# 55 matmuls of zeros between the first steps of a windowed-attention and feed-forward kernel

## The chip, the cores and the metric

The kernel runs on one core of one Trainium2 chip. The metric is the time of one execution in device microseconds; lower is better. The engines of the core are PE (matmuls; PEld is its weight load), DVE (vector), ACT (scalar, activations), POOL (GpSimd) and SP (which here only issues transfers). Each engine works through its own instructions in the order in which the program gives them, and waits on semaphores for the others.

## What is computed

```python
scores = (q @ k.T) / sqrt(64)                   # per batch (8) and head (8), 576 positions
scores = where(abs(i - j) <= 32, scores, -1e9)  # a window of 32 to each side
attn   = softmax(scores) @ v
x      = attn, heads side by side               # 4608 x 512
h      = x @ w_in                               # 512 x 2048
out    = max(0.01 * h, h) @ w_out               # 4608 x 512
```

## The kernel before

Attention is done in items: item i is one batch, one half of its positions (288) and one pair of heads (p), so eight items make a batch. An item goes around the engines like this: `score(i)` (PE, into the PSUM tile `ps`), `exps(i)` (ACT, reads `ps`, line 308), `masked(i)` (DVE or POOL, line 316), `sums(i)` (PE, into `s`, line 338), `inverse(i)` (DVE reciprocal, line 348), `product(i)` (PE, into `x`, line 363 in the first batch) and `scaled(i)` (DVE, into `xT`, line 387). Four items of one half make 288 columns of `xT` over all heads. On these the feed-forward part runs: `h_mms` (line 401) against `w_in`, the leaky ReLU on ACT (line 412), and `o_tile` (line 459) against `w_out`.

From the second batch on, a planner interleaves the attention of the next items with the matmuls of lines 401 and 459. The opening, that is the first batch, is written out by hand instead, line by line (525 to 649), and this list is the order of the instructions on every engine. In it the queries and keys of the first batch come in by eight transfers from the POOL queue (two for each pair of heads), are transposed by PE (`transpose_first`, line 208) and copied out by DVE or ACT (`evict_first`, line 143). The feed-forward part of the first half begins inside the opening: `h_chunk(c)` multiplies what `scaled(c)` has just finished, `h_open(f)` starts a further tile of 128 of the 2048 columns, and `h_close(f)` is its ReLU. With `h_first(1)` (line 651) the second half begins.

There is one `ps` tile, and every score uses it:

```python
ps = scps.tile([128, 1024], FP32)
P0 = 512 - HALF                                 # HALF is 288, so P0 is 224
by_n = ps[:, P0:P0 + 2 * HALF].rearrange("p (n t) -> p n t", n=2)  # score(i) writes here
nc.scalar.activation(out=e, in_=ps[:, P0:P0 + 2 * HALF], func=AF.Exp, scale=scale)  # exps
eng.memset(ps[:, 512:512 + HALF], 0.0)          # fill(V): columns 512 to 799
```

Columns 0 to 223 are read by nobody. `keep_busy(ps, 0, n)` writes there: n matmuls of the weights `ones_bd` with `busy`, a 128x224 tile of zeros (line 471). The kernel before calls it once, with 14, as PE's first work.

Of the kernel before, what the change touches and what calls it, by code (L numbers as in the profile page):

```python
# [16 lines left out]
def kernel(  # L17
# [91 lines left out]
    def load_v(b, p, engs=(nc.sync, nc.sync)):  # L109

        cast = engs[0] is nc.gpsimd
        if not cast:
            vf[b, p] = fload.tile([128, NB, D], FP32, name=f"vf{p}")
        for a, r in enumerate(HEADS):
            to = vf[b, p][r] if not cast else v0b[r, p] if b == 0 else vbd[b % 2][r, p, :, r]
            engs[a].dma_start(  # L116
                out=to, in_=v[b, 2 * p + a].rearrange("(c p) d -> p c d", p=64),
            )
# [68 lines left out]
    ps = scps.tile([128, 1024], FP32)  # L187
# [14 lines left out]
    def transpose_first(b, p, which):  # L202

        src = (q0b, k0b)[which == "k"]
        tp = mmps.tile([128, ROW, 64], BF16, name="tp", tag="mm")
        for c in range(ROW):
            for r in HEADS:
                nc.tensor.transpose(tp[r, c], src[r, p, c], ident[r, r])  # L208
        trans[b, p, which] = tp.rearrange("p c i -> p i c")

    def evict_first(b, p, which, eng):
        if which == "q":
            if b not in qT:
                qT[b] = attn.tile([128, NPAIR, S], BF16, name="qT")
            to = qT[b][:, p]
        else:
            to = kTs[b, p] = kt.tile([128, S], BF16, name="kT")
        copy_to(eng, to.rearrange("p (i c) -> p i c", c=ROW), trans.pop((b, p, which)))

    def value_first(b, p, eng):  # L220
        copy_to(eng, v0b[:, p], vf[b, p])
# [48 lines left out]
    def where(i):  # L270
        return i // 8, (i // 4) % 2, i % 4

    def score(i):
        b, hf, p = where(i)
        if b == 0:
            by_n = ps[:, P0:P0 + 2 * HALF].rearrange("p (n t) -> p n t", n=2)
            for n_, blocks in enumerate(WIN[hf]):
                for blk, i0, n in blocks:
                    lo, hi = 2 * i0, 2 * (i0 + n)
                    for r in HEADS:  # L280
                        nc.tensor.matmul(  # L281
                            by_n[r, n_, lo:hi], kTs[b, p][r, 64 * blk:64 * blk + 64],
                            qT[b][r, p, hf * HALF + lo:hf * HALF + hi], start=True, stop=True,
                        )
        elif b < NATURAL:
            by_n = ps[:, P0:P0 + 2 * HALF].rearrange("p (n t) -> p n t", n=2)
            for n_, blocks in enumerate(WIN[hf]):
                for blk, i0, n in blocks:
                    lo, hi = 2 * i0, 2 * (i0 + n)
                    nc.tensor.matmul(  # L290
                        by_n[:, n_, lo:hi], kbd[b % 2][:, p, blk],
                        qT[b][:, p, hf * HALF + lo:hf * HALF + hi], start=True, stop=True,
                    )
        else:
            by_c = qT[b][:, p].rearrange("p (c i) -> p c i", c=2)
            for n_, blocks in enumerate(WIN[hf]):
                for blk, i0, n in blocks:
                    nc.tensor.matmul(  # L298
                        ps_v[:, n_, :, i0:i0 + n], kbd[b % 2][:, p, blk],
                        by_c[:, :, hf * EVEN + i0:hf * EVEN + i0 + n], start=True, stop=True,  # L300
                    )
        if b > 0:
            exps(i)
            masked(i, nc.vector if i in ON_DVE else nc.gpsimd)

    def exps(i):
        e = attn.tile([128, 2 * HALF], BF16, name="e")
        nc.scalar.activation(out=e, in_=ps[:, P0:P0 + 2 * HALF], func=AF.Exp, scale=scale)  # L308
        probs[i] = e

    def masked(i, eng):
        b, hf, p = where(i)
        e = probs[i]
        pr = prob[:, i % NPROB]
        allowed = mask_first[hf] if b < NATURAL else mask[hf].rearrange("p n c i -> p n (c i)")
        eng.tensor_mul(  # L316
            pr.rearrange("p n c i -> p n (c i)"), e.rearrange("p (n t) -> p n t", n=2), allowed,
        )
        probs[i] = [pr, None, None, None]
# [9 lines left out]
    def sums(i):  # L329

        b, hf, p = where(i)
        pr, both = probs[i][:2]
        s = xps.tile([128, HALF], FP32, name="s")
        if both is not None:
            nc.tensor.matmul(s, ones_bd, both, start=True, stop=True)  # L335
        else:
            for n in range(2):
                nc.tensor.matmul(
                    s, ones_bd, pr[:, n].rearrange("p c i -> p (c i)"),
                    start=(n == 0), stop=(n == 1),  # L340
                )
        probs[i][2] = s
        if b > 0:
            inverse(i)
# [6 lines left out]
    def product(i):  # L351

        b, hf, p = where(i)
        pr = probs[i][0]
        x = xps.tile([128, HALF], FP32, name="x")
        x_v = x.rearrange("p (c i) -> p c i", c=2)
        flat = pr.rearrange("p n c i -> p n (c i)")
        parts = [(n_, *block) for n_ in range(2) for block in WIN[hf][n_]]
        if b == 0:
            for n_, blk, i0, n in parts:  # L360
                lo, hi = 2 * i0, 2 * (i0 + n)
                for r in HEADS:
                    nc.tensor.matmul(  # L363
                        x[r, lo:hi], v0b[r, p, blk], flat[r, n_, lo:hi],
                        start=(blk == parts[0][1]), stop=(blk == parts[-1][1]),
                        skip_group_check=True,
                    )
        else:
            for n_, blk, i0, n in parts:
                lo, hi = 2 * i0, 2 * (i0 + n)  # L370
                nc.tensor.matmul(  # L371
                    x[:, lo:hi] if b < NATURAL else x_v[:, :, i0:i0 + n], vbd[b % 2][:, p, blk, :],
                    flat[:, n_, lo:hi] if b < NATURAL else pr[:, n_, :, i0:i0 + n],
                    start=(blk == parts[0][1]), stop=(blk == parts[-1][1]),
                    skip_group_check=True,
                )
        probs[i][3] = x
# [7 lines left out]
    def scaled(i):  # L385
        r, x = probs.pop(i)[2:]
        nc.vector.tensor_mul(place(i), x, r)  # L387
# [28 lines left out]
    def h_chunk(c):  # L416
        for f in range(4):
            if c == 0:
                opened[f] = mmps.tile([128, 512], FP32, name="mm", tag="mm")
            h_mms(0, f, opened[f], (c,))  # L420

    def h_open(f):
        opened[f] = mmps.tile([128, 512], FP32, name="mm", tag="mm")
        h_mms(0, f, opened[f], range(DMC))

    def h_close(f):
        h_out(0, f, opened.pop(f))
# [39 lines left out]
    def keep_busy(t, lo, n, start=False):  # L467


        for _ in range(n):  # L470
            nc.tensor.matmul(
                t[:, lo:lo + 224], ones_bd, busy, start=start, stop=False,
                skip_group_check=True,
            )
# [42 lines left out]
    def load_w_in(f0, f1):  # L517
        nc.gpsimd.dma_start(out=w_in_bf[:, :, f0:f1], in_=w_in_r[:, :, f0:f1])
# [4 lines left out]

    V, G, A = nc.vector, nc.gpsimd, nc.scalar
    qT[0] = attn.tile([128, NPAIR, S], BF16, name="qT")
    keep_busy(ps, 0, 14, True)
    fill(V)
    transpose_first(0, 0, "k")
    evict_first(0, 0, "k", V)
    transpose_first(0, 0, "q")  # L530
    evict_first(0, 0, "q", A)
    transpose_first(0, 1, "k")
    score(0)
    evict_first(0, 1, "k", V)
    spread(A, GAP + 32, 2)
    load_v(0, 1, (G, G))
    transpose_first(0, 1, "q")
    exps(0)
    value_first(0, 0, V)
    transpose_first(0, 2, "k")  # L540
    evict_first(0, 1, "q", A)
    spread(V, 0, 3)
    masked(0, V)
    load_v(0, 2, (G, G))
    transpose_first(0, 2, "q")
    evict_first(0, 2, "k", V)
    sums(0)
# [3 lines left out]
    transpose_first(0, 3, "k")  # L551
    exps(1)
    load_v(0, 3, (G, G))
    transpose_first(0, 3, "q")
    evict_first(0, 3, "k", A)
    score(2)
# [3 lines left out]
    masked(1, V)  # L560
    exps(2)
    scaled(0)
    sums(1)
    load_w_in(512, 1024)
    score(3)
    inverse(1)
    product(1)
    masked(2, G)
    exps(3)
    score(4)  # L570
    masked(3, G)
    exps(4)
    scaled(1)
    sums(2)
    product(2)
    inverse(2)
    score(5)
    load_w_in(1024, 1536)
    exps(5)
    masked(4, G)  # L580
    score(6)
    scaled(2)
    sums(3)
    h_chunk(0)
    load_w_in(1536, 2048)
# [6 lines left out]
    h_chunk(2)  # L592
    load_w_out(0)
    scaled(3)
    sums(4)
    exps(7)
    h_chunk(3)
    inverse(4)
    masked(7, G)
    product(4)  # L600
    h_close(0)
    h_close(1)
    h_open(4)
    load_w_out(1)
    h_close(2)
# [164 lines left out]
```

## Time and profile before

| | |
|---|---|
| median of 3 runs | 317.73 us (317.68, 317.73, 318.78) |
| the profiled execution, its own time | 319.02 us |
| its span, first to last instruction | 317.3 us |
| what lies around the span | 1.7 us |
| mean granted TensorE clock over the span | 0.984 |
| busy, PE / DVE / POOL / ACT | 306.0 / 218.9 / 187.7 / 167.5 us |

Busy time of PE is modelled from pipelined matmuls, so a busy PE is not necessarily PE at its peak. A line of the timeline reads: start and length in us, engine, line of the kernel, operation, what it writes and reads, shape, count, and in brackets the idle time of the engine before it with what ended it. A window's line gives the busy time of each engine in that stretch, then the granted clock of PE (1.00 is full speed), then the mean share of busy transfer engines and GB/s.

### The profile page before, as it was taken

The page shows a single profiled execution, that of the slowest core. Times are in us where ns is not written, and L with a number is a line of the kernel's source. Part 1 is how long each engine was busy: PE and PEld are TensorE (multiplying, and loading weights), DVE is VectorE, ACT ScalarE, POOL GpSimd, SP SyncE. Part 2 cuts the span into 40 slices and gives each one's busy share as a digit, 9 for nine tenths or more (in the row PEclk, how much of TensorE's full clock was granted, in tenths as well). Part 3 has the DMA queues.
Part 4 walks back from the last instruction along what each step waited for, and adds up shares of the span by engine and source line. Part 5 has one row for each costly group of instructions (what it writes and reads, how often), then busy time and mean ns, then how long its engine had stood idle before and what let it go on. Part 6 is the DMA issues. An engine that isn't in the chain of part 4 may idle for free.

```text
span 317.3 us, 6932 instructions
## 1 busy us (share of the span) xinstructions
PE 306.0 (96%) x2692; PEld 204.6 (64%) x2714; DVE 218.9 (69%) x267; ACT 167.5 (53%) x370; POOL 187.7 (59%) x258
## 2 busy tenths in 40 slices
PE   5889999999999999999999999999999999999996
PEld 4657755674755858585765858576765858576653
DVE  2879758699765996788655997688755988565100
ACT  2636755472743828274652828375552837464531
POOL 8989984536356866686546866686647866330000
PEclk9579999999999999999999999999999999999999
DMA  7999999969997994499635995599733450000102
GB/s 130 136 183 207 206 144 237 200 157 235 223 193 184 213 215 118 100 241 208 149 74 152 212 229 134 75 225 232 163 76 107 110 68 35 34 35 1 66 24 77
DMA packets 107313, 46.09 MB, mean 145 GB/s; under 512 B 68752, under 2 KB 102800, under 8 KB 107280
## 3 DMA queue, kind: packets, MB, share of 16 engines
q1 hardware_dynamic: 91936, 37.91, 58.3%
q0 software_dynamic: 14752, 7.59, 18.1%
q8 instruction: 21, 0.34, 0.5%
q10 hardware_dynamic: 592, 0.15, 0.2%
q14 instruction: 12, 0.10, 0.1%
HBM read 36.70 MB, written 9.44 MB: 145 GB/s over the span
## 4 chain that ended last, share of the span: by engine, by line
PE 77%; POOL 10%; DVE 5%; DMA 4%; issue 2%; ACT 1%; SPq 0%; DVEq 0%; ACTq 0%; POOLq 0%
PE mm L459 33%; PE mm L401 33%; PE x L371 4%; PE ps L298 3%; DVE r L348 2%; DMA kf<-in_k_dram 2%; POOL vbd L657 2%; PE s L335 2%; POOL vbd L116 2%; DMA qb<-in_q_dram 2%; POOL prob L316 2%; POOL kb L99 1%; POOL qb L99 1%; PE ps L281 1%; DVE both L326 1%
## 5 line engine op out<-in xcount | busy, mean ns | idle before, releaser
L348 DVE RECIPROCAL r<-s 128x288 f32<-128x288 f32 x64 | 125.2, 1956 | 53.3 <-PE s L335 50.7
L401 PE MATMUL mm<-xT,w_in_bf 128*128 128x288 bf16 x1024 | 135.0, 288 | 0.1
L459 PE MATMUL mm<-w_out_bf,gT 128*128 128x512 bf16 (+2 forms) x570 | 129.5, 373 | 1.3 <-issue 0.2
L412 ACT ACTIVATE gT<-mm 128x288 bf16<-128x288 f32 x256 | 101.5, 410 | 27.1 <-PE mm L401 10.3
L401 PEld LDWEIGHTS <-w_in_bf 128*128 128x128 bf16 x1024 | 98.6, 98 | 25.7 <-issue 0.5
L316 POOL TENSOR_TENSOR prob<-e,mask 128x576 bf16<-128x576 bf16 x48 | 61.3, 1278 | 83.8 <-issue 40.7
L459 PEld LDWEIGHTS <-gT 128*128 128x128 bf16 x592 | 55.8, 98 | 58.0
L464 ACT ACTIVATE o_sb<-mm 128x512 f32<-128x512 f32 (+2 forms) x37 | 21.7, 586 | 91.1 <-PE mm L459 91.1
L308 ACT ACTIVATE e<-ps 128x576 bf16<-128x576 f32 x64 | 41.4, 647 | 17.9 <-PE ps L298 7.4
L387 DVE TENSOR_TENSOR xT<-x,r 128x288 bf16<-128x288 f32 x64 | 29.2, 457 | 7.1 <-PE x L363 0.9
L235 POOL CAST vbd<-vf 64x576 bf16<-64x576 f32 x48 | 33.1, 690 | 1.4
L262 DVE COPY kbd<-kT 64x576 bf16<-64x576 bf16 x48 | 31.2, 650 | 0.3
L230 POOL CAST kb<-kf 96x384 bf16<-96x384 f32 x48 | 27.1, 590 | 1.8 <-DMA kf<-in_k_dram 1.8
L230 POOL CAST qb<-qf 96x384 bf16<-96x384 f32 x48 | 24.4, 535 | 4.4 <-DMA qf<-in_q_dram 3.9
L326 DVE TENSOR_TENSOR both<-prob 128x288 bf16<-128x288 bf16 x52 | 21.7, 417 | 3.2 <-POOL prob L316 2.5
L371 PE MATMUL x<-prob,vbd 128*128 128x96 bf16 (+1 forms) x280 | 22.6, 212 | 0.6 <-DVE xT L387 0.6
L371 PEld LDWEIGHTS <-vbd 128*128 128x128 bf16 x280 | 18.0, 98 | 3.8 <-DVE xT L387 0.7
L298 PEld LDWEIGHTS <-kbd 128*128 128x128 bf16 x240 | 15.5, 98 | 6.9
L298 PE MATMUL ps<-qT,kbd 128*128 128x128 bf16 (+2 forms) x240 | 19.3, 212 | 0.0
L335 PE MATMUL s<-both,ones_bd 128*128 128x288 bf16 x52 | 14.9, 286 | 0.2
L316 POOL TENSOR_TENSOR prob<-e,wide 128x576 bf16<-128x576 bf16 x8 | 10.2, 1276 | 5.3 <-ACT e L308 5.1
L141 ACT ACTIVATE qT<-tp 128x576 bf16<-128x576 bf16 x7 | 4.5, 649 | 7.4 <-PE tp L208 7.4
(51 smaller groups left out, 110.4 us busy)
## 6 DMA issues: line engine op xcount, KB each, us to landing
out_dram<-o_sb SPq DMA_DIRECT2D x35, 256.0 KB, 3.9
vf<-in_v_dram SPq DMA_DIRECT2D x49, 144.0 KB, 3.5
qf<-in_q_dram SPq DMA_DIRECT2D x24, 288.0 KB, 4.3
kf<-in_k_dram SPq DMA_DIRECT2D x24, 288.0 KB, 4.7
w_in_bf<-in_moe_w_in_dram POOLq DMA_DIRECT2D x4, 512.0 KB, 8.1
w_out_bf<-in_moe_w_out_dram POOLq DMA_DIRECT2D x4, 512.0 KB, 8.8
kb<-in_k_dram POOLq DMA_DIRECT2D x4, 144.0 KB, 4.6
qb<-in_q_dram POOLq DMA_DIRECT2D x4, 144.0 KB, 4.8
```

What stands on the lines that cost most here:

```text
L230: nc.gpsimd.tensor_copy(out=dst[:, p, 3 * c:3 * c + 3], in_=by_c[c])
L235: nc.gpsimd.tensor_copy(out=vbd[b % 2][r, p, :, r], in_=vf[b, p][r])
L262: nc.vector.tensor_copy(out=to.rearrange("p n (m c) -> p n c m", c=2), in_=kT[r].rearrange("p (c n m) -> p n c m", c=2, n=NB),)
L298: nc.tensor.matmul(ps_v[:, n_, :, i0:i0 + n], kbd[b % 2][:, p, blk], by_c[:, :, hf * EVEN + i0:hf * EVEN + i0 + n], start=True, stop=True,)
L308: nc.scalar.activation(out=e, in_=ps[:, P0:P0 + 2 * HALF], func=AF.Exp, scale=scale)
L316: eng.tensor_mul(pr.rearrange("p n c i -> p n (c i)"), e.rearrange("p (n t) -> p n t", n=2), allowed,)
L348: nc.vector.reciprocal(r, probs[i][2])
L371: nc.tensor.matmul(x[:, lo:hi] if b < NATURAL else x_v[:, :, i0:i0 + n], vbd[b % 2][:, p, blk, :], flat[:, n_, lo:hi] if b < NATURAL else ...
L387: nc.vector.tensor_mul(place(i), x, r)
L401: nc.tensor.matmul(h[:, 0:HALF], w_in_bf[:, c, ts(f, 128)], xT[:, c, ds(g * HALF % RING, HALF)], start=(c == 0), stop=(c == DMC - 1),)
L412: nc.scalar.activation(out=to, in_=x, func=AF.Prelu, alpha=0.01)
L459: nc.tensor.matmul(o[:, lo:hi], gT[:, f, ds(128 * j % RING, 128)], w_out_bf[:, f, lo:hi], start=(f == 0), stop=(f == FFC - 1),)
```

## The change

The first call of `keep_busy` issues 17 matmuls instead of 14, and sixteen further calls with 55 matmuls in all stand between steps of the hand-written opening. These calls leave `start` at False. Nothing else changes its place. In order:

```diff
-    keep_busy(ps, 0, 14, True)
+    keep_busy(ps, 0, 17, True)
     fill(V)
     transpose_first(0, 0, "k")
     evict_first(0, 0, "k", V)
+    keep_busy(ps, 0, 3)
     transpose_first(0, 0, "q")
     evict_first(0, 0, "q", A)
+    keep_busy(ps, 0, 4)
     transpose_first(0, 1, "k")
     score(0)
...
+    keep_busy(ps, 0, 6)
     transpose_first(0, 1, "q")
     exps(0)
     value_first(0, 0, V)
+    keep_busy(ps, 0, 5)
     transpose_first(0, 2, "k")
...
+    keep_busy(ps, 0, 3)
     transpose_first(0, 2, "q")
     evict_first(0, 2, "k", V)
     sums(0)
     evict_first(0, 2, "q", A)
     score(1)
     inverse(0)
     transpose_first(0, 3, "k")
     exps(1)
     load_v(0, 3, (G, G))
+    keep_busy(ps, 0, 3)
     transpose_first(0, 3, "q")
     evict_first(0, 3, "k", A)
     score(2)
     product(0)
...
     exps(2)
     scaled(0)
+    keep_busy(ps, 0, 6)
     sums(1)
     load_w_in(512, 1024)
+    keep_busy(ps, 0, 1)
     score(3)
     inverse(1)
     product(1)
     masked(2, G)
     exps(3)
+    keep_busy(ps, 0, 4)
     score(4)
     masked(3, G)
     exps(4)
     scaled(1)
+    keep_busy(ps, 0, 4)
     sums(2)
+    keep_busy(ps, 0, 1)
     product(2)
     inverse(2)
     score(5)
     load_w_in(1024, 1536)
     exps(5)
     masked(4, G)
+    keep_busy(ps, 0, 6)
     score(6)
     scaled(2)
+    keep_busy(ps, 0, 3)
     sums(3)
     h_chunk(0)
     load_w_in(1536, 2048)
     exps(6)
     inverse(3)
     h_chunk(1)
     masked(5, G)
     score(7)
     product(3)
     h_chunk(2)
     load_w_out(0)
     scaled(3)
+    keep_busy(ps, 0, 2)
     sums(4)
     exps(7)
+    keep_busy(ps, 0, 1)
     h_chunk(3)
...
     h_close(1)
+    keep_busy(ps, 0, 3)
     h_open(4)
```

## The prediction

> **What bounds the kernel now.** I read the page first: the busy shares and the chain of waits.
>
> ```profile
> PE 306.0 (96%) x2692; PEld 204.6 (64%) x2714; DVE 218.9 (69%) x267; ACT 167.5 (53%) x370; POOL 187.7 (59%) x258
> PE 77%; POOL 10%; DVE 5%; DMA 4%; issue 2%; ACT 1%; SPq 0%; DVEq 0%; ACTq 0%; POOLq 0%
> ```
>
> PE is busy 96% of the span and makes up 77% of the chain. Windows of 5 us show it busy for 4.79 to 5.00 us in each from 20 to 50 us, so little later can absorb a late opening: what PE loses before 22 us is lost at the end. Next the windows, cut where the granted clock changes (the last but two columns: clock, DMA share, GB/s; PE busy stands first).
>
> ```profile
> 1.51:4.93 3.42, 2.80 (x14) 1.94 (x14) 0.60 (x4) 1.28 (x1) 3.35 (x8) 1.00 0.91 169
> 4.93:8.34 3.41, 1.93 (x80) 1.54 (x82) 1.34 (x2) 0.95 (x2) 3.15 (x9) 1.00 1.08 154
> 8.34:11.76 3.42, 2.55 (x62) 1.76 (x56) 2.40 (x6) 1.84 (x4) 3.42 (x6) 0.50 1.54 168
> 11.76:15.17 3.41, 3.41 (x82) 2.78 (x80) 3.08 (x4) 2.33 (x5) 2.90 (x4) 0.50 1.45 91
> 15.17:18.58 3.41, 1.79 (x42) 1.17 (x39) 3.31 (x3) 1.90 (x3) 3.25 (x4) 1.00 1.20 192
> 18.58:22.00 3.42, 3.42 (x28) 2.08 (x29) 2.78 (x3) 0.65 (x1) 3.31 (x4) 0.50 1.10 164
> ```
>
> The clock moves in steps of 3.41 us, and each stretch follows how busy PE was in the one before: after 57%, 75% and 52% busy it is half, after 82% (the zeros of line 471) and 100% it is full. (The first stretch is shown as 1.00, but its 14 matmuls of 224 columns start 0.187 us apart, against 0.1225 for 288 columns at full clock, 36 in 4.41 us in the chain: it ran at half.) So work of zeros does count, and three half stretches lie in the opening. The last, full of work, costs 1.7 us.
>
> Then the timelines of PE, ACT and DVE, for what each wait is and what may be put into it.
>
> ```profile
> 14.41 0.66 PE L281 MATMUL ps<-qT,kT 64*64 64x96 bf16 x10
> 15.82 0.43 PE L281 MATMUL ps<-qT,kT 64*64 64x64 bf16 x10 [0.40 <-ACT e L308]
> 16.53 0.42 PE L338 MATMUL s<-prob,ones_bd 128*128 128x288 bf16 x2 [0.29 <-DVE r L348]
> 18.56 0.66 PE L281 MATMUL ps<-qT,kT 64*64 64x64 bf16 x10 [0.80 <-ACT e L308]
> ```
>
> ```profile
> 13.67 0.67 ACT L308 ACTIVATE e<-ps 128x576 bf16<-128x576 f32 x1
> 15.12 0.65 ACT L308 ACTIVATE e<-ps 128x576 bf16<-128x576 f32 x1 [0.78 <-PE ps L281]
> 16.34 0.65 ACT L308 ACTIVATE e<-ps 128x576 bf16<-128x576 f32 x1 [0.58 <-PE ps L281]
> 17.86 0.65 ACT L308 ACTIVATE e<-ps 128x576 bf16<-128x576 f32 x1 [0.87 <-PE ps L281]
> ```
>
> ```profile
> 4.51 0.30 DVE L224 MEMSET ps<- 128x288 f32 x1 [1.02 <-PE ps L471]
> ```
>
> The last line decides this case. `fill` writes columns 512 to 799 of `ps`, the zeros columns 0 to 223, and still `fill` waits for the last of the zeros: accesses to `ps` are ordered by the tile, not by its columns. So zeros that stand behind `exps(i)` in the program must wait until ACT has read `ps`, and an `exps` behind zeros must wait for them. They don't run in the waits for ACT, they run after them.
>
> [...]
>
> **The change, part by part.** A matmul of zeros costs 0.187 us at half clock; at full, 0.1225 x 224/288 = 0.095. Going from 64-row to 128-row matmuls and back costs about 0.1 each (10.76 to 11.36 us: two sums of 0.24 each take 0.60 before the next score).
>
> The bare round is from one `exps` to the next: 0.65 of ACT, 0.05 to the score, 0.52 from the score's start to the next `exps`, 1.22 in all, which is 15.12 to 16.34. At full clock the zeros then make of it:
> - 2 to 3: 6 zeros 0.57, a switch 0.1, `sums(1)` 0.25, 1 zero and a switch 0.19: 2.25 to 2.35, against 1.45 now. `sums(1)` did not have to wait for `exps(2)` before.
> - 3 to 4: 4 zeros and a switch 0.48: 1.70, against 1.22.
> - 4 to 5: 0.48, `sums(2)` 0.25, a zero and switches 0.3, `product(2)` 0.24: 2.3, against 1.52. Here `sums(2)`, which ran beside `exps(4)`, is pushed behind it.
> - 5 to 6: 6 zeros and switch 0.67, and 3 zeros with two switches before `sums(3)`, for which `exps(6)` must now wait, 0.4: 2.3, against 1.46.
>
> The four rounds lose 0.85 + 0.48 + 0.78 + 0.84 = 2.95 us. Ahead of them: the three more at the start end at 4.56 + 0.39, before the first transpose at 5.00 (and `fill` ends at 5.37, before DVE's copy at 5.51): nothing. The 3 and 4 before `q` of pair 0 and `k` of pair 1 lie in waits of 0.26 and 1.05 us for their transfers: nothing to 0.1. The 6, 5, 3 and 3 up to `score(2)` cost 17 x 0.095 = 1.6 plus switches, of which the waits for transfers (0.78 before 9.37) and a full clock for 8.34 to 13 give back most: `exps(2)` comes 0.4 late. Behind them: the two chunks from 19.61 at full clock rather than half give back 8 x 0.12 = 0.95; the 2 before `sums(4)` hold up `exps(7)`, and the 1 behind it waits for `exps(7)`, where `h_chunk(3)` waited for nothing: 0.65 us of ACT and 0.1; the 3 before `h_open(4)` lie in its wait for a buffer, 0 to 0.3. Sum: 0.4 + 2.95 - 0.95 - 0.5 (`product(3)` and the next, at full clock too) + 0.75 = 2.65 us, with a full clock throughout.
>
> That is the floor; it won't be held. A round of 2.3 us leaves PE idle for about 0.8 (ACT's 0.65 and the ways there and back), so it is 65% busy, below the 75% after which the clock was half. At half clock the same round is 2.3 + 7 x 0.09 + 0.4 = 3.3, and 76% busy: between 75% and 82%, so undecided. Half and full will take turns. A half stretch costs 3.41 x 0.76 / 2 = 1.3 us; I count two of them behind 13 us (the floor has taken back those of before): 2.65 + 2.7 = 5.3 us. Bounds: none (2.65), all of them (four or five more, +9).
>
> Nothing else pays for it or hides it: no transfer moves in its queue, though POOL's `load_w_in` and `load_w_out` stand behind `masked` on POOL and come later with it, by as much as PE.
>
> Against its own execution (319.02 us) this is 324.3. The median, 317.73, lies 1.3 below that execution, and one run in three was at 318.78: where the 3.41 us steps fall differs between executions. I take the shift at the median and forecast 323.0 us; own range 320.3 to 327.
>
> **Rivals.**
> - The clock stays full (2.65 alone): 320.4. The zeros add work to each stretch, and 82% was enough. [...]
> - Nearly always half: each stretch from 13 us on stays below what is needed, since PE stands still in every `exps`. 326.7.
> - Absorbed: PE's later waits (1.46 us idle from 20 to 80 us) shrink and only 1 us is left: 318.8. Against it: those pieces are 0.2 to 0.45 us, and follow PE's own order.
> - Faster: the zeros do not wait for `exps`, as the line of `fill` would have to be a peculiarity of the first call. Then PE is fed in its waits of 0.40, 0.29 and 0.80 us, the clock is full from 8.34 us, the half stretches give back 1.7 (the last) and little from the first two (9.37 and 10.14 us wait for transfers); the zeros that overhang cost some 0.3 to 0.5. 316.4 us. It decides at one point: whether zeros behind `exps(2)` start before ACT ends. That the change does nothing at all can't be: 58 matmuls are 5.5 us at full clock and PE waits for some 4.2 us in all before 19 us.
>
> **How the numbers follow.** Main case 0.52; clock full 0.22; nearly always half 0.13; absorbed 0.07; faster 0.06. 0.5% (1.6 us), about what a measurement of this kernel can tell from no change, puts the limits at 316.1 and 319.3. Faster by more: half of the last case, 0.03. Within: the other half, the absorbed case, and 0.02 of the full clock on an unlucky reference, 0.12. Slower: 0.85. The range 319.4 to 327.0 leaves out the faster and absorbed cases and the top of the half-clock case.
>
> **What would show it.** In the changed profile zeros stand directly behind the end of each `exps`, with PE idle before them "<-ACT e"; the starts of the third to sixth `exps` lie 1.7 to 3.3 us apart; `sums(2)` waits for zeros, not for the reciprocal; the granted clock still shows half stretches after 8.34 us; `h_chunk(0)` begins 3 to 6 us later than 19.61. It is wrong if zeros overlap with an `exps` on ACT, or if the clock is 1.00 from 8.34 us on with `h_chunk(0)` before 19.6.

## The result, and the profile after

The changed kernel takes 321.71 us (median of 5, 321.66 to 322.86) against 317.80 for the kernel before: a ratio of 1.0129 with a 95% interval of 1.0106 to 1.0152, so slower by about 1.3%. The profiled execution took 321.70 us with a span of 320.0 (before: 319.02 and 317.3). Executions more than 1.5% above the fastest of their kernel are called slow and left out of the ratios below; among them are e2's profiled one (1814.88 us) and three of e4's six, its profiled one (329.99 us) included.

The forecast of 323.0 was of the right sign and the result lies in its range, but it got there by a term that is not there: the clock.

From the page of the changed kernel, the granted clock in 40 slices; nothing in it is below 9 (before: 9, 5, 7, 9 at the start). Its record begins at 4.36 us; the zeros ahead of that start 0.187 us apart, against 0.095 from 9.21 us on, so they ran at half.

```profile
PEclk9999999999999999999999999999999999999999
```

Two of its stretches of 3.41 us, in which PE was busy for only 2.17 and 2.11 us (64% and 62%), with the full one that follows the first (the stretch behind the second, from 21.42 us, is full too):

```profile
11.19:14.60 3.41, 2.17 (x71) 1.78 (x70) 2.73 (x3) 2.92 (x5) 2.69 (x4) 1.00 1.65 101
14.60:18.01 3.41, 2.58 (x43) 2.02 (x43) 2.26 (x2) 0.85 (x2) 2.45 (x2) 1.00 1.14 172
18.01:21.42 3.41, 2.11 (x33) 1.66 (x32) 2.13 (x3) 1.10 (x2) 3.38 (x5) 1.00 1.20 187
```

The timeline of PE in the changed kernel, over three rounds:

```profile
14.62 0.74 PE L471 MATMUL ps<-busy,ones_bd 128*128 128x224 bf16 x6 [0.80 <-ACT e L308]
15.20 0.41 PE L338 MATMUL s<-prob,ones_bd 128*128 128x288 bf16 x2
15.44 0.26 PE L471 MATMUL ps<-busy,ones_bd 128*128 128x224 bf16 x1
15.63 0.43 PE L281 MATMUL ps<-qT,kT 64*64 64x96 bf16 x10
16.80 0.54 PE L471 MATMUL ps<-busy,ones_bd 128*128 128x224 bf16 x4 [0.50 <-ACT e L308]
18.51 0.54 PE L471 MATMUL ps<-busy,ones_bd 128*128 128x224 bf16 x4 [0.80 <-ACT e L308]
18.89 0.41 PE L338 MATMUL s<-prob,ones_bd 128*128 128x288 bf16 x2
```

PE is idle first, until ACT has read `ps`, and only then come the zeros, with the useful work behind them. The waits were not filled, and `sums(1)` and `sums(2)`, which did not wait for ACT before, now stand behind zeros that do. The list of waits (us in total, times, longest) has both directions, seven groups of zeros that wait for `exps` and two `exps` that wait for zeros:

```profile
PE ps L471 <- ACT e L308: 4.3, 7, 0.8
ACT e L308 <- PE ps L471: 3.6, 2, 2.0
```

The timeline of ACT in the changed kernel; these are `exps(2)` to `exps(7)`:

```profile
13.93 0.65 ACT L308 ACTIVATE e<-ps 128x576 bf16<-128x576 f32 x1
16.10 0.65 ACT L308 ACTIVATE e<-ps 128x576 bf16<-128x576 f32 x1 [1.53 <-PE ps L281]
17.81 0.65 ACT L308 ACTIVATE e<-ps 128x576 bf16<-128x576 f32 x1 [1.06 <-PE ps L281]
20.10 0.65 ACT L308 ACTIVATE e<-ps 128x576 bf16<-128x576 f32 x1 [1.64 <-PE ps L281]
22.39 0.65 ACT L308 ACTIVATE e<-ps 128x576 bf16<-128x576 f32 x1 [1.64 <-PE ps L471]
25.00 0.65 ACT L308 ACTIVATE e<-ps 128x576 bf16<-128x576 f32 x1 [1.97 <-PE ps L471]
```

The rounds are 2.17, 1.71, 2.29 and 2.29 us long. At the end of the opening the delay is handed on whole. The line to compare is the eighth and last reciprocal of the first batch in DVE's timeline, before and then after:

```profile
31.17 1.96 DVE L348 RECIPROCAL r<-s 128x288 f32<-128x288 f32 x1 [0.15 <-PE s L338]
```

```profile
33.80 1.96 DVE L348 RECIPROCAL r<-s 128x288 f32<-128x288 f32 x1
```

From its start to the end of the span it is 286.15 us before (317.31 - 31.17) and 286.17 after (319.97 - 33.80). So the opening alone decides, and the start of this one instruction tells what it lost: 2.63 us.

### The profile page after: what moved, and what is told of

Its sections match the earlier page's. It is cut to its first block, busy times and chain, and to the rows that moved or that the text cites. A ratio compares the mean times of both kernels' runs of the same rounds, so it can differ in the third digit from the quotient of the medians.

```text
span 320.0 us, 7048 instructions
## 1 busy us (share of the span) xinstructions
PE 308.4 (96%) x2750; PEld 207.7 (65%) x2772; DVE 219.3 (69%) x267; ACT 167.8 (52%) x370; POOL 187.7 (59%) x258
## 4 chain that ended last, share of the span: by engine, by line
PE 78%; POOL 9%; DVE 5%; DMA 3%; issue 3%; ACT 1%; SPq 0%; ACTq 0%; DVEq 0%; POOLq 0%
PE mm L459 33%; PE mm L401 32%; PE x L371 4%; PE ps L298 3%; POOL vbd L673 2%; DVE r L348 2%; DMA kf<-in_k_dram 2%; PE s L335 2%; PE ps L471 2%; POOL prob L316 2%; POOL vbd L116 2%; ACT e L308 1%; DMA kb<-in_k_dram 1%; POOL w_out_bf L522 1%; DVE both L326 1%
## 5 line engine op out<-in xcount | busy, mean ns | idle before, releaser
L471 PE MATMUL ps<-busy,ones_bd 128*128 128x224 bf16 x72 | 11.1, 287 | 5.8 <-ACT e L308 4.3
```

## The experiments

The table gives the start of that last reciprocal, the span, and the difference, all from the profiled execution. The time is the median of the executions that the ratio uses; ratios are to the kernel before in the same job.

| kernel | us | ratio, 95% interval | last reciprocal | span | span less reciprocal |
|---|---|---|---|---|---|
| before, first profile | 317.73 | | 31.17 | 317.31 | 286.15 |
| changed | 321.71 | 1.0129, 1.0106 to 1.0152 | 33.80 | 319.97 | 286.17 |
| e1, only groups behind an `exps` | 321.02 | 1.0098, 1.0077 to 1.0118 | 33.02 | 319.19 | 286.17 |
| e2, only the other groups | 317.90 | 1.0013, 0.9987 to 1.0039 | | | |
| e3, zeros in other tiles | 319.20 | 1.0036, 1.0018 to 1.0053 | 30.95 | 317.51 | 286.56 |
| e4, a quarter of the array | 328.18 | 1.0286, 1.0232 to 1.0341 | 42.14 | 328.29 | 286.15 |
| e5, before again | 317.58 | 0.9994, 0.9977 to 1.0011 | 30.95 | 317.11 | 286.16 |
| e6, sums ahead of the zeros | 321.45 | 1.0121, 1.0104 to 1.0138 | 34.01 | 320.18 | 286.17 |
| e7, fewer zeros, in other tiles | 317.62 | 0.9995, 0.9984 to 1.0006 | 30.09 | 316.24 | 286.15 |
| e8, e2 again | 320.05 | 1.0068, 1.0049 to 1.0088 | 31.19 | 317.35 | 286.16 |
| e9, groups behind an `exps` doubled | 325.25 | 1.0221, 1.0195 to 1.0247 | 37.77 | 323.94 | 286.17 |
| e10, one zero in each of these groups | 320.93 | 1.0097, 1.0061 to 1.0133 | 31.94 | 318.09 | 286.15 |

**e1 and e2: which groups carry the loss.** The calls of the changed kernel are divided in two; both keep the first 17.

```diff
-    keep_busy(ps, 0, 3)  # e1: out, with the 4, 6, 3, 1, 1, 3, 2 and 3 that are not behind an exps
     keep_busy(ps, 0, 5)  # e1: stays, with 3, 6, 4, 4, 6 and 1; e2 has it the other way round
```

> The first call of 17 and, of the others, only the seven groups (29 zeros) that stand behind an exps in the program: 5, 3, 6, 4, 4, 6 and 1. Theory A (the loss is new waits of zeros for ACT's exps, in each round): these seven carry it, and more than half of the 3.9 us stays: with the clock full, rounds of 2.15, 1.7, 2.0 and 1.9 us, 319.8 us; idle time of PE before line 471 ended by ACT e about 4 us as in the changed kernel. Rival B (every zero costs its own 0.095 us, wherever it stands): 29 of 58 zeros, so half of 3.9, 319.8 us too, but PE's idle time ended by ACT e would not be what changes against the kernel before. The two part in the next kernels.

> The first call of 17 and only the other ten groups (26 zeros), none of them the first thing behind an exps that is still running. Theory A: they lie in waits for transfers or cost at most their own time off the chain: 317.4 us with a full clock, up to 1.5 more if half stretches come back. Rival B: half of 3.9 us stays, 319.7.

e1 keeps 3.2 of the 3.9 us with 29 of the 55 zeros of the new calls. Its rounds, from `exps(2)` to `exps(6)`, are 2.08, 1.71, 2.19 and 1.90 us, close to what was expected; the 319.8 us was 1.2 too low, and in its profile the clock was half once, from 8.69 to 12.10 us. At its median e2 is not to be told from the kernel before. That a zero costs its own time wherever it stands (rival B, 319.7 for e2) is out. e2 is less clean than its median looks: its executions spread from 317.2 to 321.5, it has no profile that can be used, and e8, below, is the same kernel.

**e3: the same zeros, another tile.** From the fourth group on the zeros go into spare columns of the tiles of `sums` and `product`, each at a point where no other engine reads that tile.

```diff
-        s = xps.tile([128, HALF], FP32, name="s")
+        s = spare("s", i)[:, 0:HALF]      # a tile of 512 columns; x in the same way
...
-    keep_busy(ps, 0, 4)
+    keep_busy_in("x", 1, 4)               # keep_busy(spare("x", 1), HALF, 4, True)
     score(4)
```

> All 58 zeros at the same places of PE's order, but from the fourth group on they go into spare columns 288 to 511 of the tiles s and x, which no engine reads at that time, so that no zeros wait for an exps and no exps for zeros. Theory A: the loss is gone, exps at most 1.5 us apart from the third to the seventh, 317.4 us. Rival B: the zeros still take 58 x 0.095 us of PE, 321.7 us or a little less.

319.20: most of the loss is gone, 1.4 us are not. No zeros wait for an `exps` in its profile, against 4.3 us in the changed kernel. The rounds are 1.50, 1.23, 1.90 and 1.23 us; the third is longer than the 1.5 expected, so the placing costs something of its own. One such cost shows on DVE (line 481 is the zeros' line here): `scaled(2)` must wait for the three zeros that went into its `x` ahead of `sums(3)`, and DVE stands idle for 0.71 us before it:

```profile
19.91 0.46 DVE L397 TENSOR_TENSOR xT<-x,r 128x288 bf16<-128x288 f32 x1 [0.71 <-PE x L481]
```

The zeros here also set `start`; that flag was not tested by itself. Another 0.41 us lie behind the opening (286.56 against 286.15), where PE waits 0.33 us at 40.82 for a transfer into `kb`.

**e7: the cleaner contrast.** Of e3's zeros only those groups stay that stood behind an `exps`, 25 of the 29 of e1, in the same places of PE's order; the start has 17 + 3 + 4 as in the changed kernel.

```diff
-    keep_busy_in("x", 2, 3)               # before scaled(2); so the 6, 3, 3, 1, 1, 2, 1 and 3
     keep_busy_in("x", 2, 6)               # stays before score(6), with 5, 6, 4 and 4
```

> The first 17 + 3 + 4 zeros in ps as in the changed kernel, then only 5, 6, 4, 4 and 6 in spare columns of s and x; dropped are the 6 before q of pair 1, the 3 before q of pairs 2 and 3, all single ones, and those before sums(3), sums(4) and h_open(4), among them the 3 that scaled(2) had to wait for. Theory A1: the 1.4 us that the kernel with all zeros elsewhere still lost were delays of the chain of reciprocals by such zeros; clock full, 317.0 to 317.8 us. Rival (the zeros of the seven groups cost their own PE time even where they wait for nothing): 318.6 us or more.

317.62, and 0.9995 (0.9984 to 1.0006): the loss is gone, as theory A1 had it; which of the dropped zeros cost e3 its 1.4 us was not parted further. PE in e7, the round from `exps(3)` (which runs from 14.65 to 15.30) to `exps(4)`:

```profile
14.44 0.41 PE L373 MATMUL x<-prob,v0b 64*64 64x96 bf16 x10
14.78 0.56 PE L481 MATMUL x<-busy,ones_bd 128*128 128x224 bf16 x4
15.35 0.43 PE L281 MATMUL ps<-qT,kT 64*64 64x64 bf16 x10
```

Here the four zeros run beside ACT, and the score follows 0.05 us behind the end of `exps(3)`; in the changed kernel the same four started 0.05 us after ACT's end. In e7, too, no zeros wait for an `exps`. Against e1 the difference is 3.4 us. That is nearly all for which tile the zeros write to, but not a pure measure of it: e1 has four zeros more behind an `exps` and lacks the 3 and 4 of the start. Its half stretch is not what parts the two, since the two executions of e1 with a mean clock of 1.000 (321.12 and 321.35 us) are no faster than the others.

**e9 and e10: the price of one zero.** The seven groups are doubled, and cut to one each.

```diff
-    keep_busy(ps, 0, 6)
+    keep_busy(ps, 0, 12)                  # e9; e10: keep_busy(ps, 0, 1)
     sums(1)
```

> The changed kernel with the seven groups behind an exps doubled (5, 3, 6, 4, 4, 6, 1 become 10, 6, 12, 8, 8, 12, 2): 29 zeros more. Theory A2 (each of these zeros lies on the chain of rounds from exps to exps, at 0.095 us): 2.75 us more at most, the 5 and the 3 partly covered by transfers, so 2.0 to 2.75: 323.7 to 324.5 us, last reciprocal 36 to 36.6 us, clock full. Rival (they lie beside DVE's reciprocals, and only the wait for ACT costs): 321.7 us.

> The changed kernel with one zero matmul in each of the seven groups behind an exps, 22 fewer; the other groups stay. The waits for ACT stay, the zeros' own time goes. Theory A2: 22 x 0.095 = 2.1 us less, 319.6 us with a full clock; with half stretches (theory C: less of the array at work) up to 1.7 more. Rival (only the wait costs): 321.7 us with a full clock.

The group of six that took 0.74 us at 14.62 in the changed kernel, in e9 with twelve, behind the same wait:

```profile
16.59 1.31 PE L471 MATMUL ps<-busy,ones_bd 128*128 128x224 bf16 x12 [0.80 <-ACT e L308]
```

In e9 the four rounds are 2.75, 2.09, 2.67 and 2.86 us: longer by 0.58, 0.38, 0.38 and 0.57 for 6, 4, 4 and 6 zeros, about 0.095 each, as the prediction put it. The time rose by 3.5 us rather than 2 to 2.75. The rounds give 1.91 of it; most of the rest lies ahead of them, for the first reciprocal starts at 13.10 instead of 11.43. There the clock of the profile was half up to 6.59 us, and five zeros more stand ahead of `k` of pair 2; how the two share it was not parted. In e10 the rounds are 1.69, 1.42, 2.00 and 1.80, shorter by 0.48, 0.29, 0.29 and 0.49 for 5, 3, 3 and 5 zeros. Its three executions with a mean clock of 1.000 took 319.83, 319.97 and 320.44 us, near the 319.6 expected; the three below 1.000 took 321.42 to 322.94. That only the wait costs is out: zeros and waits both do.

**e6: DVE's reciprocals or the rounds?** The same 58 zeros, but `sums(1)`, `sums(2)` and `sums(3)` go ahead of the zeros that stood before them.

```diff
-    keep_busy(ps, 0, 6)
     sums(1)
     load_w_in(512, 1024)
-    keep_busy(ps, 0, 1)
+    keep_busy(ps, 0, 7)
     score(3)
```

> The changed kernel with the same 58 zeros, but in three places sums(i) goes ahead of the zeros that stood before it: 7 zeros behind sums(1), 5 behind sums(2), 3 behind sums(3). No zeros leave PE's order, and the rounds from exps to exps stay as long. Theory A1 (what sets the end of the opening is DVE's chain of reciprocals, started late by sums that wait for exps): inverse(1) starts at 14.5 instead of 15.64, the last reciprocal 2 us earlier than 33.80, 319.7 us. Theory A2 (the rounds of PE and ACT themselves set it): unchanged, 321.7 us.

321.45, so A1 fell. From the first to the second reciprocal it is indeed 2.82 us rather than 4.21, but from the first to the last it is 21.88 against 22.37 (compared from the first, which comes 0.70 later here, with the clock half up to 7.13 us): the later `sums` stand behind `score(4)` and `score(6)` in PE's order, and these keep waiting for the lengthened rounds. So the rounds of PE and ACT set the pace.

**e4: the zeros on a quarter of the array.** They use 64x64 of it, for the same number of columns.

```diff
-                t[:, lo:lo + 224], ones_bd, busy, start=start, stop=False,
+                t[0:64, lo:lo + 224], ones_bd[0:64, 0:64], busy[0:64], start=start, stop=False,
```

> All groups as in the changed kernel, but each matmul of zeros uses 64 x 64 of the array (rows and columns 0 to 63) instead of 128 x 128, and so a quarter of it, for the same 224 columns. What the prediction missed is the full clock from 4.36 us on. Theory C (the gate counts how much of the array works): a quarter of the activity, half stretches come back, and 322.5 to 325 us. Theory D (it counts only the time in which PE is fed): clock 1.000 and 321.7 us, some tenths less for fewer switches between 64-row and 128-row matmuls.

The three executions that the ratio uses took 324.47, 328.18 and 328.54 us, the last two above the 322.5 to 325 that theory C gave; these two show recorded half stretches (mean clock 0.990 and 0.984). The profile is of an execution of 329.99 us. Its timeline of PE has the group that took 0.54 us at 18.51 in the changed kernel, behind the same wait:

```profile
22.86 0.90 PE L471 MATMUL ps<-busy,ones_bd 64*64 64x224 bf16 x4 [0.81 <-ACT e L308]
```

It takes 0.90, as at half clock, and the first full clock in e4's record begins at 32.16 us, behind the first 128-row matmuls of line 401 (at 29.07); what the windows show before that, 1.00, is an empty record: two `sums` matmuls take 0.66 us at 28.61 and 0.42 at 33.07. PE was not idle there (window of e4):

```profile
5.00:10.00 5.00, 4.98 (x95) 4.77 (x96) 2.36 (x5) 1.49 (x3) 4.74 (x11) 1.00 1.17 180
```

Busy for 4.98 of 5.00 us and still half: a busy PE did not bring the full clock here, and the same groups on 128x128 had it from 4.36 us on. So theory D is out.

The traces of the two kernels show what stood ahead of the steps of the clock. In the kernel before, the stretches from 4.93 to 8.34 us (57% busy; the recorded matmuls that start in it stream 5568 columns on 64x64 and none on 128x128), from 8.34 to 11.76 (75%; 3520 and 576) and from 15.17 to 18.58 (52%; 3648 and 576) were followed by half clock, and the one from 11.76 to 15.17 (100%; 6400 and 576) by full. In the changed kernel those from 11.19 to 14.60 (64%; 5568 and 672) and from 18.01 to 21.42 (62%; 2176 and 3040) were followed by full. So the busy share does not part half from full, nor do the columns on 128x128 alone. What does was not shown.

**e5 and e8: second profiles.** The kernel before, and e2, unchanged.

> The kernel before, unchanged, for a second profile. Theory A: its median runs (317.8) have fewer half stretches on the chain than its first profile (319.02); if this execution is near the median, the last reciprocal of the first batch starts about 1.2 us before 31.17, and there is one half stretch less after 15 us. Rival: the difference of 1.2 us lies elsewhere, and the reciprocals start where they did.

> The ten groups that do not stand directly behind an exps, once more, for a profile of an ordinary execution. Theory A1: the reciprocals start within 0.5 us of those of the second profile of before, and no zeros wait for ACT for more than 0.3 us. Theory C (zeros on the whole array hold the clock): fewer half stretches than before, though not none.

e5's profile shed little light: its execution took 318.84 us, again among the slower ones of the kernel before (its executions lie between 317.1 and 319.5), and again with a half stretch late in the opening (18.23 to 21.64 us). The list of mean clocks says more. A half stretch of 3.41 us takes about 0.005 off the mean of a span of 317 us. Of the 54 executions of the kernel before that the ratios above were taken against, 36 have a mean clock of 1.000, so no recorded half stretch, and took 317.11 to 318.59 us, median 317.59. The other 18 took 317.70 to 319.46; the five of them at 0.984, like the first profile with its three half stretches, have a median of 318.88. The mean is blind to a half clock ahead of the first recorded step (in the first profile the zeros from 1.57 us on start 0.187 us apart, and the window shows 1.00).

e8 is the same kernel as e2 and measured 320.05. Its reciprocals start within 0.4 us of e5's and no zeros wait for an `exps`, as expected. Its profile has the clock full from 4.27 to 17.92 and half to 21.33, and an `exps(7)` that waits 2.90 us, the last part of it for the two zeros ahead of `sums(4)`. The eight executions of e2 with a mean clock of 1.000 took 317.19 to 318.02 us; the six of e2 and e8 below that took 319.05 to 321.51. So the ten groups cost next to nothing in an execution without a recorded half stretch, and those with one were 1.0 us longer or more.

## Why the prediction was right, and where it was not

- **Order by the tile.** Right, and the heart of it: the one line on `fill` foretold seven waits of zeros for `exps`. e3 and e7, in which the zeros write other tiles and none waits for an `exps`, show that it is the tile.
- **The sum at full clock.** The rounds were put at 2.25 to 2.35, 1.70, 2.3 and 2.3 us; they are 2.17, 1.71, 2.29 and 2.29. `exps(2)` came 0.26 late, not 0.4. `h_chunk(3)` begins at 25.80 instead of 23.15, 2.65 late, and the span is 2.7 us longer: the floor of 2.65 to the decimal. The decimal is luck: up to `exps(6)` the loss was 3.07 rather than 3.35, and what follows gave back 0.42 rather than 0.70. The parts listed for the round from 4 to 5 also add up to 2.49 with the bare round, not to the 2.3 written there. Of the signs, `h_chunk(0)` came 2.76 us late, just short of the 3 to 6.
- **Half and full will take turns (+2.7; two stretches of 1.3 would be 2.6).** This step failed. In the profile the clock was full from 4.36 us to the end of the opening and beyond, and all five executions have a mean clock of 1.000. The step took the busy share of PE for what decides the next stretch, with a limit between 75% and 82%. In the changed kernel two stretches of 3.41 us with a share below that (64% and 62%, shown above) were followed by full ones. e4 shows that it matters which part of the array the zeros use: on 64x64 they left the clock of the profile at half up to 32.16 us, with PE busy for 4.98 us of the 5.00 from 5 to 10 us, and the time at 328.18 us. What decides the next stretch was not shown. The rival with the full clock had this step right.
- **The shift at the median.** The step from 319.02 to 317.73 was taken off the changed kernel too, and it should not have been. Its profiled execution (321.70) is its median, with the same mean clock as the others. So the 3.9 us are 2.7 from profile to profile, and 1.2 by which the median execution of the kernel before is better than the profiled one. The mean clocks point to the reason: most executions of the kernel before, those around its median among them, have no recorded half stretch, and its first profile has three. What the steps cost one by one is not shown, for both profiles of it fell among its slower executions. Two wrong terms, 2.7 too much and 1.3 too little, met near the result.
- **Nothing later absorbs it.** Right: 286.15 to 286.17 us remain after the last reciprocal in all kernels but e3 (286.56), for openings that end 12 us apart.
- **Faster rival.** Its condition was that zeros don't wait. Where that was made true (e7), the clock was full from 5.80 us and the last reciprocal began at 30.09 rather than 31.17 or 30.95, but the median still stayed that of the kernel before, not 316.4. The gain was counted from half stretches that most executions of the kernel before do not show. PE in e7 also waited 0.45 us for `w_in` at 19.64, and 0.28 us for DVE at 13.27.

## What to carry to other kernels

Before filling a wait of an engine, look up whom the filler itself has to wait for: work in a tile that the awaited engine is reading ran after the wait here, not in it (seven waits, 4.3 us), and one line of a profile that shows two accesses to different columns waiting for each other was enough to know. Filler belongs into a tile that nobody reads at that time, and even there it can hold up the next reader (0.71 us in e3). And before paying for a clock that is held, see how often it drops: the profile had three half stretches, but two in three executions of the kernel before had none on record, so even zeros that waited for nobody gained nothing at the median.

## What the runs showed of the hardware

- The clock did not follow the busy share of PE. In the changed kernel, stretches of 3.41 us that were 64% and 62% busy were followed by full clock; in the kernel before, one that was 75% busy was followed by half.
- The same zeros on 64x64 of the array instead of 128x128 left the clock of e4's profile at half up to 32.16 us, with PE 4.98 us busy of the 5.00 from 5 to 10 us, and cost 6.5 us (328.18 to 321.71).
- The first recorded full stretch began at 4.27 us (e8), 4.36 (changed), 4.93 (before) and 7.13 (e6), and the same kernel (e2, e8) measured 317.2 to 321.5 us, the executions with a mean clock of 1.000 at most 318.02.
- Ahead of the first recorded step the views showed 1.00 where the clock was half, and e4's profile, half up to 32.16 us, has a mean clock of 1.000; the spacing of the matmuls told (in the changed kernel 0.187 us for 224 columns on 128x128 ahead of 4.36 us, and 0.095 from 9.21 on).
